# First tile of a convolution + ELU feed-forward kernel: x loaded in 128 packets of eight tokens, transposed in token order, with its own halo load and the taps built in one pass

## The chip, the cores and the metric

The kernel runs on one core of one Trainium2 chip. The metric is the device time of one execution in microseconds (us). A profiled execution also gives a span, which is 1.7 to 2.1 us shorter than the time of that execution. The profiler writes TensorE as PE (its weight loads as PEld), VectorE as DVE, ScalarE as ACT, GpSimd as POOL and SyncE as SP. "L787" is line 787 of the kernel that was profiled, and the same code has another line number in the changed kernel.

## The reference, cut to what matters

```python
x: (8, 4096, 192)   weight: (8 heads, 7 taps)   w_in: (192, 2048)   w_out: (2048, 192)
w   = softmax(weight, axis=-1)
att = causal depthwise convolution of x over the sequence, 7 taps, 24 channels a head
h   = att @ w_in                                  # 32768 tokens
g   = where(h > 0, h, exp(min(h, 0)) - 1)         # ELU
out = g @ w_out                                   # float32
```

## The kernel before: the parts that the change and the argument touch

The tokens are worked in 32 tiles of 1024. From the second tile on, the convolution is a matmul with a banded matrix `Tm` in which the seven taps of a head stand along a diagonal ("band convolution"). `Tm` needs a detour through DRAM: zeros are written (`conv_band<-zw`), the taps are written along the diagonal (`conv_band<-wprb`), the block is read back (`Tm<-conv_band`). Each of the three waits for the one ahead of it.

```python
# SyncE
W(s_zw, 1)
W(s_xs, 32)                                  # x of the first tile has landed
sy.dma_start(band..., zw[:, :]).then_inc(s_band, 16)
W(s_band, 16); W(s_set, 8)                   # zeros are in DRAM, wprb is made
sy.dma_start(diagonal, wprb[:, :, :]).then_inc(s_band, 16)
W(s_band, 32)
sy.dma_start(Tm[:, :, :], band[:, :, PAD : PAD + CW]).then_inc(s_band, 16)
```

Since `Tm` comes late, the first tile goes another way: x is loaded with four tokens in a partition, cast to bf16 (`xb`), transposed on PE against the identity, copied out of PSUM to `xT`, and convolved by seven matmuls with diagonal matrices (`taps`).

```python
# ScalarE: x of the first tile in two loads, 128 rows of 3 KB each; SUP = 1024, GS = 512, XI = 4
for g in range(2):
    eng.dma_start(xs[:, g, :, :], x_flat[GS*g : GS*(g+1), :].rearrange("(p i) d -> p i d", i=XI))
# VectorE: one pass a tap
for tap in range(KSIZE):
    v.tensor_scalar(out=taps[:, tap, :], in0=ident[:], scalar1=wch[:, tap:tap+1], ..., op0=ALU.mult)
for j in (0, 1, 3):                           # copies out of PSUM; ScalarE has j = 2
    v.tensor_copy(xT[:, j, HALO:HALO+GS].rearrange("p (t i) -> p i t", i=XI), H[...])
# ... cut ...
EARLY_CONV = (6, 7, 9, 10)                    # steps at which the second tile is convolved
CONV_AT = (14, 18, 23, 25)                    # the same for the later tiles
```

PE works through a fixed list: warm-up matmuls, four transposes (`t`), three diagonal convolutions (`d`), and then steps n = 0, 1, ... of H matmuls (`h`, att @ w_in), output matmuls (`o`, g @ w_out) and band convolutions (`c`). An item that waits holds everything behind it. GpSimd issues the loads of the weights and of the later tiles, on its software queue, in this order, ahead of its first clamp of the ELU:

```python
load_w_in(0, 0); load_w_in(0, 1); load_w_in(1, 0); load_w_in(1, 1)
load_w_out(0)
for gr in range(2): load_x(1, gr)
load_w_out(1)
for gr in range(2): load_x(2, gr)
```

## Time and profile before

| | before |
|---|---|
| median of three runs | 735.63 us (735.42 to 736.54) |
| span of the profiled execution (which took 733.98 us) | 732.0 us |
| first H matmul | 20.12 us |
| `Tm` landed | 27.48 us |
| first band convolution on PE | 27.56 us |
| one tile in the steady part | 21.86 us |

The busy line of the page gives time and share of the span. The clock row has one digit for each fortieth of the span; 9 is 90% or more of the full rate.

```profile
PE 720.5 (98%) x11829; PEld 679.3 (93%) x11830; DVE 641.2 (88%) x1048; ACT 677.0 (92%) x1285; POOL 670.3 (92%) x1116
...
PEclk8999999999999999999999999999999999999999
```

PE is busy almost always, and from about 50 us on the chain of work that ended last is PE alone, but for about 12 us of GpSimd work near 660 us. The change touches the first 20 us, so the question is what there starts last. This is the head of that chain in order of time (start, duration, what):

```profile
0.80 0.42 ACTq L398
1.25 7.21 DMA xs<-in_x_dram
8.55 7.70 DMA conv_band<-zw
16.26 7.36 DMA conv_band<-wprb
23.63 3.85 DMA Tm<-conv_band
27.56 0.28 PE H L762
```

The casts, transposes, taps and the whole first tile are absent. The chain goes over DMAs, which end at the first band convolution (L762). The list of waits has the wait at that place (us in total, times, longest):

```profile
PE H L762 <- DMA Tm<-conv_band: 0.9, 1, 0.9
```

So in this execution PE had done all its work ahead of the convolution and stood for 0.9 us. The work that the change is about, in the timeline (start, duration, engine, line, operation, out<-in; in brackets the idle time before, and what ended it; the lines between these are left out):

```profile
8.27 2.26 DVE L639 TENSOR_SCALAR taps<-ident,wch 128x128 bf16<-128x128 bf16 x7
9.26 1.35 PE L712 MATMUL H<-ident,xb 128*128 128x128 bf16 x12 [2.79 <-ACT xb L577]
9.80 2.64 DVE L648 CAST xT<-H 128x512 bf16<-128x512 f32 x3
10.65 1.30 ACT L588 ACTIVATE xT<-H 128x512 bf16<-128x512 f32 x1 [0.49 <-PE H L712]
12.69 4.43 PE L740 MATMUL H<-xT,taps 128*128 128x512 bf16 x10 [1.61 <-DVE xT L648]
20.12 1.07 PE L787 MATMUL H<-att,w_in 64*128 64x512 bf16 x6
```

From 11.5 to 18.3 us the granted clock was 0.50. The columns of the windows view are the stretch, its length, the busy time of each engine with its number of instructions, the granted clock, the share of the DMA engines and GB/s:

```profile
12.00:14.00 2.00, 1.31 (x4) 0.50 (x5) 0.62 (x3) 0.00 (x0) 1.96 (x3) 0.50 1.07 249
14.00:16.00 2.00, 2.00 (x6) 0.66 (x5) 0.00 (x0) 0.13 (x1) 0.00 (x0) 0.50 1.20 210
```

### The profile page before, as it was taken

The page shows a single profiled execution, that of the slowest core. Times are in us where ns is not written, and L with a number is a line of the kernel's source. Part 1 is how long each engine was busy: PE and PEld are TensorE (multiplying, and loading weights), DVE is VectorE, ACT ScalarE, POOL GpSimd, SP SyncE. Part 2 cuts the span into 40 slices and gives each one's busy share as a digit, 9 for nine tenths or more (in the row PEclk, how much of TensorE's full clock was granted, in tenths as well). Part 3 has the DMA queues.
Part 4 walks back from the last instruction along what each step waited for, and adds up shares of the span by engine and source line. Part 5 has one row for each costly group of instructions (what it writes and reads, how often), then busy time and mean ns, then how long its engine had stood idle before and what let it go on. Part 6 is the DMA issues. An engine that isn't in the chain of part 4 may idle for free.

```text
span 732.0 us, 27565 instructions
## 1 busy us (share of the span) xinstructions
PE 720.5 (98%) x11829; PEld 679.3 (93%) x11830; DVE 641.2 (88%) x1048; ACT 677.0 (92%) x1285; POOL 670.3 (92%) x1116
## 2 busy tenths in 40 slices
PE   6999999999999999999999999999999999999998
PEld 2479999999999999999999999999999999999997
DVE  3799899889899889899889899889899889898993
ACT  3799999999999999999999999999999999999993
POOL 7799999999999999999999999999999999999892
PEclk8999999999999999999999999999999999999999
DMA  9746355534466534445534555533545634635212
GB/s 175 82 52 94 72 94 86 85 51 92 75 93 84 76 69 86 74 93 85 96 51 83 79 89 85 96 59 74 84 83 86 95 62 71 92 76 83 70 34 66
DMA packets 135114, 59.18 MB, mean 81 GB/s; under 512 B 101072, under 2 KB 134224, under 8 KB 134992
## 3 DMA queue, kind: packets, MB, share of 16 engines
q1 hardware_dynamic: 89984, 38.86, 23.6%
q0 software_dynamic: 44448, 17.58, 23.0%
q8 instruction: 92, 1.51, 0.9%
q10 hardware_dynamic: 560, 0.98, 0.4%
q14 instruction: 30, 0.25, 0.1%
HBM read 36.19 MB, written 25.45 MB: 84 GB/s over the span
## 4 chain that ended last, share of the span: by engine, by line
PE 92%; DMA 4%; POOL 2%; ACT 2%; DVE 0%; issue 0%; ACTq 0%; DVEq 0%; SPq 0%
PE H L810 52%; PE H L787 37%; PE H L762 3%; POOL E L556 1%; ACT E L597 1%; DMA conv_band<-zw 1%; DMA conv_band<-wprb 1%; DMA xs<-in_x_dram 1%; DMA Tm<-conv_band 1%; ACT csb L593 0%; POOL xg L484 0%; ACT osb L601 0%; DVE gT L670 0%; DVE osb L661 0%; ACTq L398 0%
## 5 line engine op out<-in xcount | busy, mean ns | idle before, releaser
L670 DVE SCALAR_TENSOR_TENSOR gT<-E,H 128x512 f16<-128x512 f32 x1024 | 633.1, 683 | 66.8 <-POOL E L556 65.3
L810 PE MATMUL H<-w_out,gT 64*128 64x192 f16 x8192 | 683.9, 243 | 0.2
L787 PE MATMUL H<-att,w_in 64*128 64x512 bf16 x3072 | 681.4, 377 | 0.6 <-ACT csb L593 0.2
L556 POOL TENSOR_SCALAR E<-E 128x512 f32<-128x512 f32 x1024 | 607.0, 612 | 48.4 <-ACT E L597 37.4
L810 PEld LDWEIGHTS H<-w_out,gT 64*128 64x128 f16 x8192 | 625.7, 94 | 21.9 <-PE H L810 2.3
L597 ACT ACTIVATE E<-H 128x512 f32<-128x512 f32 x1024 | 593.6, 601 | 29.1 <-PE H L787 3.4
L787 PEld LDWEIGHTS H<-att,w_in 64*128 64x128 bf16 x3072 | 275.0, 93 | 7.6 <-ACT csb L593 1.8
L762 PE MATMUL H<-xg,Tm 64*112 64x240 bf16 x496 | 92.5, 266 | 1.2 <-DMA Tm<-conv_band 0.9
L593 ACT ACTIVATE csb<-H 112x480 bf16<-112x480 f32 x124 | 69.8, 563 | 0.0
L601 ACT ACTIVATE osb<-H 128x384 f32<-128x384 f32 x127 | 61.7, 486 | 7.5 <-PE H L810 7.4
L762 PEld LDWEIGHTS H<-xg,Tm 64*112 64x112 bf16 x496 | 57.8, 126 | 5.0 <-DMA Tm<-conv_band 1.2
L484 POOL DMA_DIRECT2D xg<-in_x_dram x63 | 56.2, 898 | 0.2 <-issue 0.2
L740 PE MATMUL H<-xT,taps 128*128 128x256 bf16 (+1 forms) x27 | 7.3, 436 | 1.8 <-DVE xT L648 1.6
L740 PEld LDWEIGHTS H<-xT,taps 128*128 128x128 bf16 x28 | 3.3, 121 | 5.6 <-issue 5.3
L588 ACT ACTIVATE att<-H 128x512 bf16<-128x512 f32 (+1 forms) x2 | 1.0, 490 | 7.7 <-PE H L740 7.7
L661 DVE COPY osb<-H 128x384 f32<-128x384 f32 x1 | 0.6, 557 | 8.4 <-PE H L810 8.4
L705 PE MATMUL H<-zw 128*128 128x512 bf16 x18 | 6.1, 484 | 1.5 <-DVE zw L608 1.5
L705 PEld LDWEIGHTS H<-zw 128*128 128x128 bf16 x18 | 2.1, 120 | 5.3 <-issue 3.0
L502 POOL DMA_DIRECT2D w_in<-in_moe_w_in_dram x12 | 6.9, 670 | 0.0
L656 DVE CAST att<-H 128x512 bf16<-128x512 f32 x1 | 0.7, 690 | 6.0 <-PE H L740 6.0
L712 PEld LDWEIGHTS H<-ident,xb 128*128 128x128 bf16 x12 | 0.7, 97 | 3.8 <-issue 3.3
L712 PE MATMUL H<-ident,xb 128*128 128x128 bf16 x12 | 1.2, 220 | 3.0 <-ACT xb L577 2.8
(32 smaller groups left out, 18.9 us busy)
## 6 DMA issues: line engine op xcount, KB each, us to landing
out_dram<-osb SPq DMA_DIRECT2D x127, 192.0 KB, 3.6
xg<-in_x_dram POOLq DMA_DIRECT2D x61, 240.0 KB, 5.1
w_in<-in_moe_w_in_dram POOLq DMA_DIRECT2D x6, 192.0 KB, 7.1
xs<-in_x_dram ACTq DMA_DIRECT2D x2, 384.0 KB, 6.3
w_out<-in_moe_w_out_dram POOLq DMA_DIRECT2D x2, 384.0 KB, 11.9
att<-csb SPq DMA_TRANSPOSE x31, 4.4
w_in<-in_moe_w_in_dram POOLq DMA_DIRECT2D x6, 64.0 KB, 5.0
conv_band<-zw SPq DMA_DIRECT2D x1, 268.0 KB, 7.7
```

Of the source, the lines that this page charges most:

```text
L484: g.dma_start(xg[0:rows, b, 2 * w0 + gr : 2 * w1 : 2, :], src).then_inc(s_x[b][gr], 16)
L502: g.dma_start(w_in[HP * half : HP * (half + 1), j, c0:c1], bass.AP(tensor=moe_w_in.tensor, offset=8 * j * FF + c0, ap=[[CPH * FF, HEADS], ...
L556: g.tensor_scalar(out=E[:, i % NE, :], in0=E[:, i % NE, :], scalar1=1.0, scalar2=0.0, op0=ALU.min, op1=ALU.max,).then_inc(s_clp)
L593: a.activation(*conv_evac(W, m), ACT.Copy).then_inc(s_ce)
L597: a.activation(E[:, i % NE, :], H[:, bank_of[item], :], ACT.Exp).then_inc(s_exp)
L601: a.activation(*out_evac(W, *item[1:]), ACT.Copy).then_inc(s_oev[item[2]])
L670: v.scalar_tensor_tensor(out=gT[:, s % NG3, q, u, :], in0=E[:, i % NE, :], scalar=1.0, in1=H[:, bank_of[item], :], op0=ALU.subtract, op1=A ...
L705: pe.matmul(H[:, bank, :], zw[:, 0:P], zw[:, 0:GS], start=True, stop=True)
L740: ins = pe.matmul(H[:, bank_of[item] + part, c0:c1], taps[:, tap, :], xT[:, j, HALO - PAD + tap + c0 : HALO - PAD + tap + c1], start=(tap ...
L762: ins = pe.matmul(H[0:CW, bank_of["c", m], 256 * q : 256 * q + UC], Tm[rows, h, :], xg[rows, s % NXB, :, CPH * h : CPH * (h + 1)].rearrang ...
L787: ins = pe.matmul(H[:, bank_of[item[:3]], :], w_in[HP * r : HP * (r + 1), j, FC * q : FC * (q + 1)], att[HP * r : HP * (r + 1), s % 2, j, ...
L810: ins = pe.matmul(acc_of(k, g)[:, D * kb : D * (kb + 1)], gT[HP * rt : HP * (rt + 1), t % NG3, q, g, t0 : t0 + P], w_out[HP * rt : HP * (r ...
```

## The change

Its intent is to bring the first tile sooner to its H matmuls. x comes in one load whose rows are 6 KB (eight tokens), so there are half as many packets. Each 64x64 block is transposed on its own part of the array and written to every eighth column of PSUM, so PSUM holds the tokens in order and the copies out of it are contiguous. The eight tokens ahead of the second half (halo) come by a 6 KB load of their own. The taps are built in one pass. Three dummy matmuls (`FILL`) keep PE busy between the transposes. Here is the core of it; declarations and semaphore bookkeeping are cut, and so are the halo's own cast and its three transposes, and that ScalarE takes over one of VectorE's copies out of PSUM.

```diff
+FILL = 1
-XI = GS // P
+XI = SUP // P
-    start_up = [("t", j) for j in range(4)] + [("d", j) for j in range(3)]
+    start_up = [("t", j) for j in (3, 0, 1, 2)] + [("d", j) for j in range(3)]
     ...
+        if what[0] == "t" and what[1] < 3:
+            pe_order.append(("w", 0, FILL))
     ...
-            return (
-                xT[:, j, HALO : HALO + GS].rearrange("p (t i) -> p i t", i=XI),
-                H[:, bank_of["t", j], :].rearrange("p (i t) -> p i t", i=XI),
-            )
+            return xT[:, j, HALO : HALO + GS], H[:, bank_of["t", j], :]
     ...
-            for g in range(2):
-                first_x(a, g)
+            a.dma_start(
+                xs[:, :, :], x_flat[0:SUP, :].rearrange("(p i) d -> p i d", i=XI)
+            ).then_inc(s_xs, 16)
     ...
-            for tap in range(KSIZE):
-                v.tensor_scalar(out=taps[:, tap, :], in0=ident[:], scalar1=wch[:, tap : tap + 1], ...)
+            v.tensor_tensor(
+                taps[:],
+                ident[:, :].unsqueeze(1).to_broadcast([P, KSIZE, P]),
+                wch[:, :].unsqueeze(2).to_broadcast([P, KSIZE, P]),
+                ALU.mult,
+            ).then_inc(s_tap)
     ...
                         for i in range(XI):
+                            for g in range(2):
+                                rows = slice(HP * g, HP * (g + 1))
+                                ins = pe.matmul(
+                                    H[rows, bank_of[item], i:GS:XI],
+                                    xb[rows, j, i, :],
+                                    ident[rows, rows],
+                                    start=(i == 0),
+                                    stop=(i == XI - 1),
+                                    tile_position=(HP * g, HP * g),
+                                )
     ...
+            sy.dma_start(xh[:, :], x_flat[GS - HALO : GS, :]).then_inc(s_xh, 16)
             W(s_zw, 1)
-            W(s_xs, 32)
+            W(s_xs, 16)
```

## The prediction

> **What bounds the kernel now.** The busy table has PE at 98%, PEld 93%, ACT 92%, DVE 88%. From about 50 us on the chain of waits is PE alone, and repeats every 21.86 us (one of 32 tiles of 1024 tokens). The change touches none of that. It touches the start, and there I ask what starts last.
>
> The chain begins with DMAs, not with PE: xs<-x 1.25 to 8.46 us, conv_band<-zw 8.55 to 16.25, conv_band<-wprb 16.26 to 23.62, Tm<-conv_band 23.63 to 27.48, then the first band convolution on PE at 27.56. In the list of waits PE waits 0.90 us for Tm (its weight load 1.2). So the first tile's path (cast, transposes, diagonal taps; first H matmul 20.12 us) already ends before Tm does. From 28 to 47 us ACT alternates with PE on the chain, and PE idles under 1 us in all there.
>
> **Removed, added, moved.**
> - x: 256 packets of 3 KB become 128 of 6 KB, one issue instead of two (0.43 us each). In windows of 0.5 us x's queue ramps from 3.3 us[...], and from 5.5 us shares the engines with w_in. The Trainium skill (DMA: Bandwidth & Descriptors, Queues, rings and completion order) says that an engine alternates between queues by packet, which larger packets would profit from. Estimate: landed near 7.0 instead of 8.46 us.
> - Taps: seven passes, 2.26 us together, become one; estimate 1.0 us.
> - Evacuation of the transposes: 1.3 us each (strided), now in token order like the 128x512 att copies: 0.69 DVE, 0.60 ACT.
> - 12 transposes of 128 columns (1.35 us with gaps) become 48 of 64: estimate 0.5 to 0.7 us a tile, plus three fill matmuls. Halo: one cast (about 0.35 us) and three small transposes.
> - The diagonal taps ran at a granted clock of 0.50 from 11.5 to 18.3 us (windows): 427 ns a matmul, not 216. Filled gaps may keep the clock.
>
> Sum: diagonal taps start near 10.3 instead of 12.66 us, first H near 15 (clock kept) to 18 (clock lost), against 20.12.
>
> **How much is on the critical path.** Little. PE takes its items in order and reaches the first band convolution about 6.3 us after the first H, thus at 21.5 to 24.5 us, and stands there until Tm lands. The saving on the first tile becomes a wait of 2.5 to 5.5 us. What counts is Tm: its chain is released by x landing, so 1.5 us earlier at first. But conv_band's transfers wait 3.4 and 3.8 us from issue to first packet behind the software queue, which is saturated until 24.5 us; Tm, issued earlier, would meet that backlog. I expect Tm about 0.9 us earlier, near 26.6.
>
> Against that: in the longer wait PE may lose its clock (the skill, TensorE: Matmul & The Clock Gate, HAM oscillation; this trace lost it at 11.5 us after 3.7 idle us in 6.8). That would cost about 2 us; I give it four in ten.
>
> **Prediction:** 735.0 us, 733.2 to 737.2 (8 in 10). Faster by over 2%: 0.01; within: 0.98; slower: 0.01.
>
> **What would show it.** Right: after's chain still starts with xs, zw, wprb, Tm; the wait of PE for Tm grows from about 1 to 3-5 us; first H before 18.5 us; time changes by what Tm's landing changes by. Wrong: Tm landing 2 us or more earlier; or no PE wait there; or the period of 21.86 us changed.
>
> **What would make it wrong.** x landing near 6 us with the DMA backlog gone sooner (up to 2 us gained); a lost clock after the wait (2 to 3 us lost); w_in or w_out landing later and holding back H.

## The result, and the profile after

| | before | after |
|---|---|---|
| median of four runs | 736.09 us (735.42 to 736.87) | 736.14 us (734.57 to 736.36) |
| span of the profiled execution | 732.0 us | 734.4 us |
| first H matmul | 20.12 us | 14.98 us |
| `Tm` landed | 27.48 us | 27.69 us |
| wait of PE for `Tm` | 0.9 us | 5.6 us |

The ratio is 0.9996, with a 95% interval of 0.9978 to 1.0014. The time is the same, although the first H matmul starts 5.1 us earlier in this pair of profiles (3.1 us in a second pair, below). These are the steps of the first tile in the timeline of the kernel after (the lines between are left out):

```profile
7.75 0.63 PE L719 MATMUL H<-ident,xb 64*64 64x64 bf16 x16 [0.18 <-ACT xb L583]
8.14 1.09 DVE L645 TENSOR_TENSOR taps<-ident,wch 128x896 bf16<-128x896 bf16 x1
9.15 0.77 DVE L653 CAST xT<-H 128x24 bf16<-128x24 f32 x2
9.31 0.60 ACT L595 ACTIVATE xT<-H 128x512 bf16<-128x512 f32 x1 [0.58 <-PE H L719]
10.31 4.74 PE L747 MATMUL H<-xT,taps 128*128 128x512 bf16 x28
14.98 1.07 PE L794 MATMUL H<-att,w_in 64*128 64x512 bf16 x6
```

Each part but the dummy matmuls, which are tested below, is seen to do what it was meant to do. The 28 diagonal matmuls took 4.74 us at full clock, where before they took 7.5 us (12.69 to 20.18) mostly at half clock. But the head of the chain is the same as before:

```profile
0.80 6.24 DMA xs<-in_x_dram
7.12 7.76 DMA conv_band<-zw
14.90 7.75 DMA conv_band<-wprb
22.67 5.02 DMA Tm<-conv_band
27.73 0.45 PE H L769
```

x landed 1.42 us earlier (7.04 against 8.46), and `Tm` was issued 0.96 us earlier, but it took 5.02 us instead of 3.85 and landed 0.21 us later. (In the second pair of profiles x landed at 6.02 against 7.42 us: the difference holds, while the landing itself moves by 1.0 us between two executions of one kernel.) PE stood in front of it:

```profile
PE H L769 <- DMA Tm<-conv_band: 5.6, 1, 5.6
```

After that wait it ran at half clock, in the windows view:

```profile
24.00:26.00 2.00, 0.00 (x0) 0.00 (x0) 0.66 (x2) 0.00 (x0) 0.00 (x0) 1.00 1.37 198
26.00:28.00 2.00, 0.27 (x3) 0.27 (x5) 0.00 (x0) 0.00 (x0) 0.00 (x0) 0.75 0.23 45
28.00:30.00 2.00, 2.00 (x16) 1.64 (x13) 0.00 (x0) 0.83 (x2) 0.15 (x1) 0.50 0.00 0
30.00:32.00 2.00, 1.98 (x13) 1.12 (x11) 1.24 (x2) 1.55 (x4) 1.23 (x3) 0.50 0.00 0
32.00:34.00 2.00, 1.93 (x16) 1.67 (x18) 1.38 (x3) 1.14 (x3) 1.08 (x2) 0.54 0.00 0
```

A mean of 0.75 over 26 to 28 us, where the two levels are 1.0 and 0.5, says that the clock fell at 27.0; the 0.54 of the last line says that it rose at 33.84. That is 6.8 us at half clock, 6.1 of them after the wait.

The span can be cut at two places that all kernels here have: the start of the first band convolution, and the start of ScalarE's first copy of an output (`osb<-H`). Before: 27.56 + 18.94 + 685.5 = 732.0. After: 27.73 + 21.10 + 685.57 = 734.4. The third term is the same, the first hardly differs, and the middle one has grown by 2.16 us in the stretch with the half clock. So two things have to be explained: why `Tm` was not earlier, and whether the half clock is the cause of those 2.16 us. And the kernel before has to be looked at again, as its profiled execution was quicker (733.98 us) than all of its timed runs.

### The profile page after: what moved, and what is told of

Its sections match the earlier page's. It is cut to its first block, busy times and chain, and to the rows that moved or that the text cites. A ratio compares the mean times of both kernels' runs of the same rounds, so it can differ in the third digit from the quotient of the medians.

```text
span 734.4 us, 27620 instructions
## 1 busy us (share of the span) xinstructions
PE 722.3 (98%) x11860; PEld 682.6 (93%) x11860; DVE 638.9 (87%) x1041; ACT 677.6 (92%) x1287; POOL 671.0 (91%) x1116
## 4 chain that ended last, share of the span: by engine, by line
PE 93%; DMA 4%; POOL 2%; ACT 1%; DVE 0%; issue 0%; DVEq 0%; SPq 0%
PE H L817 53%; PE H L794 37%; PE H L769 3%; POOL E L555 1%; DMA conv_band<-zw 1%; DMA conv_band<-wprb 1%; DMA xs<-in_x_dram 1%; DMA Tm<-conv_band 1%; ACT E L604 1%; POOL xg L483 0%; ACT csb L600 0%; ACT osb L608 0%; DVE gT L675 0%; DVE osb L666 0%; DVEq L371 0%
## 5 line engine op out<-in xcount | busy, mean ns | idle before, releaser
L817 PE MATMUL H<-w_out,gT 64*128 64x192 f16 x8192 | 685.4, 243 | 0.7 <-DMA w_out<-in_moe_w_out_dram 0.6
L604 ACT ACTIVATE E<-H 128x512 f32<-128x512 f32 x1024 | 593.9, 601 | 36.1 <-PE H L794 10.3
L710 PE MATMUL H<-zw 128*128 128x512 bf16 x21 | 8.2, 522 | 1.5 <-DVE zw L615 1.5
L747 PE MATMUL H<-xT,taps 128*128 128x512 bf16 (+1 forms) x28 | 4.7, 325 | 0.0
```

The source lines that it names most:

```text
L604: a.activation(E[:, i % NE, :], H[:, bank_of[item], :], ACT.Exp).then_inc(s_exp)
L710: pe.matmul(H[:, bank, :], zw[:, 0:P], zw[:, 0:GS], start=True, stop=True)
L747: ins = pe.matmul(H[:, bank_of[item] + part, c0:c1], taps[:, tap, :], xT[:, j, HALO - PAD + tap + c0 : HALO - PAD + tap + c1], start=(tap ...
L817: ins = pe.matmul(acc_of(k, g)[:, D * kb : D * (kb + 1)], gT[HP * rt : HP * (rt + 1), t % NG3, q, g, t0 : t0 + P], w_out[HP * rt : HP * (r ...
```

## The experiments

**Theory.** The start ends with `Tm`. `Tm` lands when the backlog of the software queue (its loads that are issued and not yet moved: weights and x of later tiles) has drained, hardly sooner when it is issued sooner. What the first tile gains becomes waiting time of PE, and a waiting PE may lose its clock on top. **Rivals.** (a) `Tm` lands late for reasons of its own (the latency of three dependent DMAs). (b) The clock is without effect, and the 2 us come from elsewhere. (c) `Tm` doesn't bound anything, and the saving is lost to ScalarE or GpSimd. Each run was made beside runs of the kernel before on the same chip; those medians are 736.52, 736.25 and 736.72 us in the three groups of four below.

### Group 1: is it the wait, and is it the clock?

**before_again** and **after_again** are the two kernels unchanged, for one more profile each.

> The kernel before, unchanged, for a second profile, because its first profiled execution (733.98 us) was below all of its timed runs (735.42 to 736.87). Theory: which stretch of the start runs at half clock differs from execution to execution. Expected: Tm lands near 27.5 us and the first band convolution starts there, with PE waiting 0 to 2 us for it; the half-clock stretch lies elsewhere than 11.5 to 18.3 us and the span is 733 to 735. Rival (nothing varies but the launch): the same stretch, and a span of 732.0.

> The kernel after, unchanged, for a second profile. Theory: Tm again lands near 27.6 us, no earlier than in the kernel before, and PE waits over 4 us for it; the span is 734.4 if the clock is lost after that wait (granted clock 0.5 for 5 to 7 us from about 26.5 us), and 732 to 732.8 if it is kept.

before_again took 735.70 us (span 733.6), after_again 736.47 (span 734.6). In before_again x landed 1.0 us earlier than in the first profile and the clock was low from 12.5 to 15.9 us only, so the first H came at 18.11 us, PE waited 3.5 us for `Tm`, and then it lost its clock as well, for 3.4 us, as these two lines show:

```profile
30.00:32.00 2.00, 1.83 (x13) 1.04 (x14) 1.38 (x2) 1.78 (x5) 1.46 (x3) 0.50 0.00 0
32.00:34.00 2.00, 2.00 (x24) 1.75 (x22) 1.38 (x2) 1.14 (x3) 0.82 (x3) 0.76 0.00 0
```

Its chain ends with the same DMAs:

```profile
7.51 8.60 DMA conv_band<-zw
16.12 7.36 DMA conv_band<-wprb
23.50 4.59 DMA Tm<-conv_band
```

`Tm` landed at 28.09 us in before_again and at 27.94 in after_again, which had issued it 2.1 us sooner (21.40). So over two profiles each, 27.48 and 28.09 stand against 27.69 and 27.94: no gain. Both kernels can lose the clock in front of the band convolution; the kernel before did in one profile of two, the kernel after in two of two.

**keep_warm** puts 24 dummy matmuls where PE waits.

```diff
+        if n == EARLY_CONV[0]:
+            warm(24)
         if n < UNTIL:
```

> The kernel after with 24 dummy matmuls (5.2 us at full clock) in the place where PE waits for Tm. They do no work that is wanted and Tm is not touched. Theory (the wait costs its own length, and then a lost clock on top of it): Tm still lands near 27.6 us, the granted clock stays 1.0 from 15 to 50 us, and the time falls by about 2 us against the kernel after, to 734.0 (span 732.2). Rival (the two us come from Tm or from other stages, the clock is without effect there): 736.1, no change.

Measured: 734.65 us (733.92 to 736.43), ratio to before 0.9978 (0.9965 to 0.9992), against 0.9996 for the kernel after. `Tm` landed at 27.51 us, the clock stayed at 1.0, the span was 732.2 us as foreseen:

```profile
21.31 6.20 DMA Tm<-conv_band
```

```profile
28.00:30.00 2.00, 1.76 (x23) 1.17 (x20) 0.28 (x1) 1.61 (x4) 0.62 (x1) 1.00 0.00 0
30.00:32.00 2.00, 1.88 (x25) 1.06 (x23) 1.69 (x3) 2.00 (x5) 1.65 (x3) 1.00 0.00 0
```

The middle term was 18.99 us, against 21.10 in the kernel after and 18.94 in the first profile of the kernel before. So rival (b) falls: with the same landing of `Tm`, and with more work on PE, the middle shrinks by 2.1 us when the clock is kept.

That size rests on the profiles. The median fell by 1.5 us, and the interval of its ratio overlaps that of the kernel after. The record also has the mean granted clock of every run, and from it the time at half clock can be estimated, as twice the missing share of the span. It is 0.999 or 1.0 in all six runs of keep_warm (at most some 2 us), 0.992 to 0.995 (an estimated 7 to 12 us at half clock) in the five of the kernel after, and 0.990 to 0.995 (7 to 15 us) in the 33 runs of the kernel before that stood beside the experiments. So the dummy matmuls kept the clock in every run, and neither kernel kept it in any of these; a mean doesn't tell at which place it was lost. And with the clock kept the six runs still spread from 733.92 to 736.43 us, the profiled one being the fastest: something else moves the time by up to 2.5 us, and that stays open.

**late_conv** convolves the second tile at later steps, so that PE has other work meanwhile.

```diff
-EARLY_CONV = (6, 7, 9, 10)
+EARLY_CONV = (9, 10, 11, 12)
```

> The kernel after with the first tile's successor convolved at steps 9, 10, 11, 12 in place of 6, 7, 9, 10, so PE has H and o work to do while Tm is on its way. Theory (the saving on the first tile is real, and only the wait for Tm at this place swallowed it): PE reaches the convolution near 25.5 us, waits under 2.5 us instead of 5.6, keeps its clock, and the time falls by 3 to 5 us, to 731 to 733, less what a later transposed att then makes H wait (up to 1.5 us). Rival (Tm does not bound the start; the first tile's saving is lost elsewhere, for instance to ACT, which is 92 percent busy): within 1 us of 736.1.

Measured: 734.82 us, ratio 0.9972 (0.9959 to 0.9985), a little below what rival (c) allows, but not the 731 to 733 of the theory. The profile, which caught the slowest of the five runs (735.64), shows three reasons. `Tm` took 7.96 us and landed at 30.08, so PE still waited 3.0 us for it; PE did lose its clock, from 31.1 to 34.5 us; and PE waited 1.1 us for the transposed att of the second tile, which now came late:

```profile
22.12 7.96 DMA Tm<-conv_band
38.40 4.56 DMA att<-csb
```

The end of that `Tm` is instructive. Between 28.0 and 29.5 us the only traffic was this, by queue (packets, MB, share of 16 engines; q0 is the software queue, q1 the one that carries `Tm`):

```profile
q0 software_dynamic: 26, 0.01, 5.3%
q1 hardware_dynamic: 27, 0.01, 3.3%
```

Read one by one from the trace, the packets of the two queues alternate strictly, 384 bytes of the software queue and 224 of `Tm`, one pair every 56 ns, far below what the 16 engines moved before. From 29.58 us, when the software queue has nothing left, the last packets of `Tm` follow each other every 13 ns. The Trainium skill (DMA: Bandwidth & Descriptors, Queues, rings and completion order) says that a copy is split over up to 16 engines and that each engine goes round the queues by packet. The strict alternation agrees. That a single engine was behind with its share is my reading of it; the trace doesn't name the engines.

### Group 2: what holds `Tm` back, and what is the first tile worth without it?

**xg2_late** moves only the two loads of the third tile's x out of the way.

```diff
-            for gr in range(2):
-                load_x(2, gr)
             for i, (n, u) in enumerate(units):
+                if i in (12, 14):
+                    load_x(2, i // 2 - 6)
```

> The kernel after with the two loads of the third tile's x (240 KB each, on the software queue) issued by GpSimd after its 12th clamp (about 24 us) instead of at 12 us. Nothing of Tm's own chain is touched. Theory (Tm lands when the software queue's backlog has drained, not when its chain began): the backlog ends near 20 us, Tm lands near 26 us or before, PE waits about 4 us instead of 5.6 to 6.1, the time falls by 1 to 2 us, to 734.1 to 735.1. Rival (Tm's landing is its own latency and the bytes of its rows): Tm lands at 27.5 or later, no change.

Measured: 733.85 us, ratio 0.9968 (0.9953 to 0.9982). `Tm` was issued at 22.29 us, about as in the kernel after (22.67), and took 3.12 us instead of 5.02:

```profile
14.64 7.64 DMA conv_band<-wprb
22.29 3.12 DMA Tm<-conv_band
```

Rival (a) falls for this last transfer: the same transfer, at the same time, lands 2.3 us sooner when the software queue has less to do. The backlog ended later than I had thought (24.2 us, not 20), and the time fell a little further than expected. PE still waited 3.2 us and lost its clock (24.5 to 31.3 us), and the middle term was 20.95 us.

**zw_early** takes away the wait of the zeros for x.

```diff
             W(s_zw, 1)
-            W(s_xs, 16)
```

> The kernel after with the zeros of the band written at once, not after x has landed. Theory: x lands up to 1 us later, which costs nothing; the taps go out near 10.5 us instead of 14.9, as soon as VectorE has made them, and Tm is issued near 18 us, inside the backlog, so it lands near 24.5 to 25.5; PE waits 2.5 to 3.5 us; 732.5 to 734.5, depending on whether the clock is kept. Rival (only the backlog's end counts): Tm lands near 27 us all the same and the time stays near 736.

Measured: 734.18 us, ratio 0.9975 (0.9960 to 0.9991). The taps went out at 10.41 us and `Tm` was issued at 18.22, as expected, but it landed at 26.96:

```profile
10.41 7.79 DMA conv_band<-wprb
18.22 8.74 DMA Tm<-conv_band
```

I had expected 24.5 to 25.5. In this profile a `Tm` that is issued 4.5 us sooner than in the kernel after lands 0.7 us sooner. The end of the backlog counts even more than I had put it. (The profile caught the slowest of the four runs, 735.46 us; the others took 733.64 to 734.40, and when `Tm` landed in them isn't known.)

The kept traces allow a direct check: when does the last packet of the backlog start, and when does `Tm` land?

| run | `Tm` issued | last packet of the backlog | `Tm` landed |
|---|---|---|---|
| before | 23.63 | 26.34 | 27.48 |
| before_again | 23.50 | 26.96 | 28.09 |
| after | 22.67 | 26.57 | 27.69 |
| after_again | 21.40 | 26.97 | 27.94 |
| xg2_late | 22.29 | 24.21 | 25.41 |
| zw_early | 18.22 | 26.93 | 26.96 |
| after_both (below) | 17.93 | 22.49 | 23.59 |

The issue moves by up to 5.7 us, and `Tm` lands 0.0 to 1.2 us after the backlog's last packet. The two kernels issue the same loads on that queue, and their backlogs end at the same time within 0.7 us. xg2_late, which only takes loads off that queue, shows that the backlog moves `Tm` and not the reverse. That is why the earlier start was worth nothing to `Tm`.

**after_both** and **before_both** make both edits in the kernel after and in the kernel before.

> The kernel after with both of these. Theory: Tm is issued near 17 us, lands near 21 to 22, before PE comes to the first convolution (21.7 us): no wait for Tm, no lost clock, so the 5.6 us of wait and the 2 us of half clock both go: 728 to 730.5. Rival (something else takes the time back): above 733.

> The kernel before with the same two edits, as the partner of after_both. Theory: with Tm out of the way the time follows the first tile, which in the kernel before reaches the first convolution near 24 to 26.5 us: 732 to 734.5, so 2.5 to 5 us more than after_both. That is what the change is worth where Tm doesn't bound. Rival (the change's first tile is worth nothing): the same time as after_both within 1 us.

Measured: after_both 731.05 us (730.38 to 732.46), ratio 0.9932 (0.9919 to 0.9945); before_both 733.50 us (732.95 to 733.92), ratio 0.9963 (0.9950 to 0.9975). before_both is within what the theory allowed, after_both 0.5 us above it. The difference is 2.45 us, just under the 2.5 to 5 that were foreseen. In before_both no wait for `Tm` is left, and the chain now runs over the first tile, that is over what the change makes faster, and then over GpSimd, which from 28.0 us also has the two moved loads to issue (0.85 and 0.82 us):

```profile
7.97 1.71 DVE taps L639 x7
9.69 1.89 DVE xT L648 x2
12.05 7.26 PE H L740 x28
21.03 6.95 POOL E L556 x12
```

So the change is worth something where `Tm` is out of the way, and nothing where it isn't. after_both still waited 1.8 us for `Tm` (landed at 23.59, when it had been expected at 21 to 22), and in the profiled run lost its clock from 23.7 to 27.2 us:

```profile
17.93 5.66 DMA Tm<-conv_band
```

Three of its six runs have a mean clock of 1.0; they took 730.38 to 731.27 us, the other three 730.83 to 732.46.

### Group 3: the rest of the wait, and the parts of the change

**three_late** also moves the second half of w_out; **before_three_late** is its partner.

```diff
-            load_w_out(1)
             ...
+                if i == 6:
+                    load_w_out(1)
                 if i in (12, 14):
```

> after_both with one more load taken out of the way of Tm: the second half of w_out (384 KB, first read at step 12) is issued after GpSimd's 6th clamp instead of before the first. Theory: the software queue's backlog ends near 20 us, Tm lands before 22 us, PE waits under 0.5 us and keeps its clock; 729 to 730.5, thus 0.5 to 2 us under after_both (731.05). Rival (the first tile or ACT bounds there already, and not Tm): 731, no change.

> The kernel before with the same three edits, as the partner of three_late. Theory: Tm did not bind in before_both any more (no wait for it there), so nothing is gained over it: 733 to 734, and 3 to 4.5 us over three_late. Rival (the change's faster first tile is worth nothing or only the 2.4 us seen before): within 2.5 us of three_late.

Measured: three_late 731.06 us (730.73 to 731.23), ratio 0.9922 (0.9908 to 0.9936); before_three_late 734.60 us, ratio 0.9971 (0.9958 to 0.9984). The wait for `Tm` is gone (it landed at 22.4 us) and the clock is kept, but the time is that of after_both, as the rival had said, though not for the rival's reasons. The list of waits of three_late shows what came in its place, and the chain between 15 and 27 us shows from where:

```profile
PE H L770 <- DVE gT L676: 1.7, 1, 1.7
```

```profile
17.58 3.49 POOL E L556 x6
21.07 0.89 POOL w_out L512
...
21.99 3.49 POOL E L556 x6
```

GpSimd spends 0.89 us on issuing the load that was moved, in the middle of its clamps; VectorE waits for the clamps, and PE for a PSUM bank that VectorE frees. A wait for DMA became a wait for the engine that issues the DMA. before_three_late pays for the same issue, and is 0.6 us slower than the 733 to 734 that I expected. The pair differs by 3.54 us; in the profiles the first band convolution comes at 24.09 and 27.17 us and the spans are 729.5 and 732.5, so the 3.1 us by which the first tile is ahead arrive at the end almost whole.

**three_late_no_fill** sets `FILL = 0`; **three_late_taps7** puts the seven passes for the taps back.

> three_late without the three dummy matmuls between the transposes. Theory of the prediction (filled gaps keep the clock): the granted clock falls to 0.5 somewhere between 10 and 16 us, the diagonal taps take up to 3 us longer, the time rises by 1 to 3 us. Rival (the earlier x and the tighter chain keep PE busy enough alone): the clock stays 1.0, the time falls by 0 to 0.8 us.

> three_late with the seven passes of VectorE for the taps put back. Theory: seven passes take 1.7 to 2.3 us where one takes 1.1, and the evacuation of the first transpose stands behind them, so the diagonal taps start 0.7 to 1.2 us later and the time rises by as much. Rival (the taps are off the path): no change.

Without the fill: 730.98 us (730.42 to 731.08), ratio 0.9919 (0.9905 to 0.9933), and in the profile the granted clock stays at 1.0 through the diagonal taps, which start at 10.40 us. The rival was right: the dummy matmuls aren't needed here. The mean clock of its five runs is 0.997 to 1.0, and 0.998 to 1.0 in the six of three_late, so some runs of either lose it for a short time, at a place that the mean doesn't tell. With seven passes: 731.62 us (730.87 to 731.83), ratio 0.9929 (0.9916 to 0.9942). The passes took 2.11 us together and the diagonal taps started 2.41 us after the first pass, against 1.93 in three_late_no_fill and 2.14 in three_late. That is 0.3 to 0.5 us, less than the 0.7 to 1.2 expected. But that profile also lost its clock for 3.4 us (from 25.7 us), so the 0.56 us between the medians can't be put down to the taps alone.

### The profiles side by side

| run | first H | wait of PE for Tm | first band conv. | half clock after it | to first output copy | to the end | span |
|---|---|---|---|---|---|---|---|
| before | 20.12 | 0.9 | 27.56 | 0 | 18.94 | 685.5 | 732.0 |
| before_again | 18.11 | 3.5 | 28.14 | 3.4 | 20.04 | 685.4 | 733.6 |
| after | 14.98 | 5.6 | 27.73 | 6.1 | 21.10 | 685.6 | 734.4 |
| after_again | 15.03 | 6.1 | 27.98 | 5.9 | 21.00 | 685.6 | 734.6 |
| keep_warm | 15.01 | none | 27.55 | 0 | 18.99 | 685.7 | 732.2 |
| xg2_late | 15.14 | 3.2 | 25.46 | 5.8 | 20.95 | 685.5 | 731.9 |
| zw_early | 15.74 | 4.7 | 27.00 | 6.2 | 21.12 | 685.5 | 733.6 |
| after_both | 15.29 | 1.8 | 23.64 | 3.4 | 19.97 | 685.5 | 729.1 |
| before_both | 19.25 | none | 26.69 | 0 | 19.66 | 685.5 | 731.9 |
| three_late | 15.79 | none | 24.09 | 0 | 19.78 | 685.6 | 729.5 |
| before_three_late | 18.88 | none | 27.17 | 0 | 19.79 | 685.5 | 732.5 |
| three_late_no_fill | 15.07 | none | 23.36 | 0 | 19.79 | 685.6 | 728.7 |
| three_late_taps7 | 15.54 | none | 23.83 | 3.4 | 20.26 | 685.6 | 729.7 |

The first band convolution, the stretch to the first output copy and the stretch to the end add up to the span. (late_conv is left out, since it convolves at other steps.) The stretch to the end is constant within 0.3 us. The one before it depends on the clock: 18.9 to 19.0 us without a loss, 20.0 to 20.3 with 3.4 us of half clock, 20.9 to 21.1 with about 6; and it is 19.7 to 19.8 without a loss where GpSimd has the moved loads to issue in it. So in these profiles the span is decided by when the first band convolution starts, plus one or two us for the clock or the moved loads.

## Why the prediction was right

It was right that the time would not change, and its main reason, the wait for `Tm`, is what the runs show. That the number came out so close is in part luck, as the last points say.

- **The bound.** "The chain begins with DMAs, not with PE", ending with `Tm`: shown by the chains of both kernels, and by xg2_late, after_both and before_both, in which the time follows when `Tm` is freed. What holds `Tm` is the end of the software queue's backlog, in both kernels alike (the table in group 2).
- **The parts.** x landed at 7.04 us (near 7.0 was predicted), the taps took 1.09 us (1.0), a tile's transposes 0.63 us (0.5 to 0.7), the copies 0.60 and 0.68 us. Diagonal taps started at 10.31 us (10.3), and the first H at 14.98 us (15 with the clock kept). For x the reason isn't shown, though: larger packets were to profit from the alternation with w_in, but in windows of 0.5 us x's bytes rise about alike in both kernels (0.15, then 0.19 MB from 4.5 us on before; 0.15, then 0.20 MB from 4.0 us on after), and its first packet started 1.0 us sooner (2.27 against 3.28 us); no run here shows a gain by the alternation. In the five profiles that have the start of the kernel after unchanged x landed between 6.0 and 7.1 us, so the 7.04 is in part luck.
- **The wait.** 2.5 to 5.5 us were predicted; 5.6 and 6.1 were measured, slightly more, since `Tm` wasn't sooner. The sign that "time changes by what Tm's landing changes by" did not hold in the first pair of profiles: `Tm` landed 0.2 us later and the span grew by 2.4, nearly all of it in the stretch with the half clock.
- **`Tm` itself was mis-sized.** The prediction had "about 0.9 us earlier, near 26.6"; it landed at 27.69 and 27.94, against 27.48 and 28.09 before. The backlog that the prediction named held it back entirely and not in part. The profile of zw_early shows how firmly: 4.5 us of lead yield 0.7.
- **The lost clock was mis-sized too.** It was given four chances in ten at about 2 us. The size holds in the profiles (2.1 us by keep_warm's; the medians show 1.5). The chance was too low: both profiles of the kernel after lost it, and by its mean clock (0.992 to 0.995) every other run lost it somewhere, the one of 734.57 us too, which was 1.5 us faster than the others for a reason that isn't known. The loss was also put down to the change alone, while before_again shows that the kernel before can lose it there too (1.1 us). And the idle time that the prediction read before the loss at 11.5 us, 3.7 us, is 3.4 us in the windows view (6.82 us, 3.46 of them busy).
- **The fill.** "Filled gaps may keep the clock" gets no support: the profile of three_late_no_fill kept it without them, and the time is the same.

The net was a change of about -0.6 us from 735.63 to 735.0; the measured ratio is 0.9996. This is where luck comes in: `Tm` gave nothing, and the kernel after lost its clock each time, which alone would have made it slower; but the kernel before, in its ordinary runs, was also slower than its first profile, and lost its clock as well.

The fastest versions are after_both, three_late and three_late_no_fill, at 731.0 to 731.1 us, 0.7 to 0.8% under the kernel before of the same rounds, which is clear of the noise. None of them is clear of the others.

## What to carry to other kernels

Before a start-up stage is made faster, look at which wait ends last where its result is first joined with another chain; here a first tile that was 3 to 5 us faster only lengthened the wait for a matrix that came by three dependent DMAs. A small transfer that is issued earlier need not land earlier beside another queue's bulk loads (here 4.5 us of lead gave 0.7); look for bulk loads that are not needed yet and can be moved, and mind what issuing them costs the engine that does it. A wait of PE can cost more than its own length, because the clock may be lost in it (2.1 us here). And a profile is one execution: compare its time with the other runs before its sizes are taken for the kernel's.

## What the Trainium skill lacked or had wrong

- **TensorE: Matmul & The Clock Gate, Why this matters for your kernels.** It advises no PE idle gaps above about 3 us. Here shorter ones lost the clock: after_both lost it at 23.7 us, at the end of a wait of 1.8 us, with 1.9 us of PE idle time in the 6.8 us up to then; three_late kept it with a wait of 1.75 us at the same place, and three_late_taps7 lost it 1.9 us after just such a wait of 1.75 us. In the waits for `Tm` the clock fell 1.8 us (after_again), 2.2 us (xg2_late), 4.1 us (zw_early) and 4.9 us (after) after PE had stopped. The length of one gap didn't decide it. The page's section on a second HAM failure mode does describe losses through frequent short idle times, but without a length.
- **The same page, Part 1.** It gives a free-running window of 3413 ns. The half-clock stretches in these profiles, read off windows of 0.25 us, lasted 3.4 (before_again, after_both), 6.8 (before, after, xg2_late) and 10.2 us (after_again), which agrees. It also says that the slow matmuls at a kernel's start vary in number from run to run. What it lacks is how far executions of one kernel can differ after the start: here two executions of the same kernel differ by 1.6 us in span (732.0 and 733.6), 1.1 us of it in the stretch where only the second was at half clock.
- **DMA: Bandwidth & Descriptors, Latency and other measured facts.** It gives about 600 ns to the first byte for DMAs issued from SyncE or ScalarE. Beside the software queue's backlog, the first packet of the taps (14 KB, issued at 16.26 us in the kernel before) started between 20.0 and 20.5 us, read off windows of 0.5 us, thus 3.7 us or more after the issue, and the whole transfer took 7.36 us. The same 224 KB `Tm` took from 3.1 us (xg2_late) to 8.7 us (zw_early). Apart from an HBM access latency of 2 us at high load, the page gives no figure for a transfer beside a saturated queue.
- **The same page, Anatomy of one DMA.** It calls the generation of descriptors on the software path "small, variable". Its table of latencies does have about 1 us to the first byte on this path, as emission overhead; what it lacks is how long the issue holds up the other work of GpSimd. In three_late the issue of the 384 KB of w_out was 0.89 us of GpSimd, in the middle of its clamps, and PE then waited 1.75 us behind them.
